# Agent attention with a squared-ReLU layer behind it: both layers, scores and transposes rewritten as pairs of 64-row matmuls

## Chip, cores and metric

The kernel runs on one core of a Trainium2 chip. The metric is device time in microseconds (us), from one launch to its end. Engines are named as in the profile: PE is TensorE's matmul stream, PEld its weight loads, DVE is VectorE, ACT is ScalarE, POOL is GpSimd, SP issues the DMAs.

## What is computed

Attention through 49 agent rows, and then a feed-forward layer on its output:

```python
a2k = sm(agents, k);  agent_v = a2k @ v          # B=4, N=12480, C=128, 49 agents
q2a = sm(q, agents);  x = q2a @ agent_v          # sm: scaled softmax along the last axis
r = np.maximum(x @ w_in, 0.0)                    # w_in 128 x 2048
out = (r * r) @ w_out                            # w_out 2048 x 128, 49920 tokens
```

All of it is float32, at float32 accuracy.

## The kernel before

**Folding.** `agent_v @ w_in` is computed once for each of the four batches (`w_make`), so that the first layer takes the 49 softmax weights of a token and not its 128 channels. Each factor is split into a high part of matmul type fp32r and the rest, low; a product is then high x high, high x low and low x high. In the program's names `hi` and `lo` are the parts of a weight, `gh` and `gl` those of the squared activation, and the columns of `pp` and `pe` hold high and low of the softmax weights side by side.

**Tiles.** Tokens come in 52 tiles of 960 (13 of each batch; `ST`), as 8 chunks of 120. The 2048 hidden columns are 16 blocks of 128 (`NF`). A step i of the main loop is one block for one tile: 832 steps, the largest part of the work.

**A step.** `mm1` forms h for two steps at once (L342-351): for each step two matmuls, one for each half of 480 tokens, over 126 rows, in which high x high, high x low and 28 of the 49 rows of low x high are stacked (L348); then, for both steps together, four matmuls over the 21 rows that are left, each in its own strip of 32 rows of the array and its own bank (L351). h of one step has two banks, 128 x 960. ACT does the ReLU (L355) and the square (L359), DVE the rounding to `gh` (L363) and the rest `gl` (L367). Four steps later (`LAG`) `mm2` adds six matmuls over 128 rows into the two banks out0 and out1, one for each half of the tokens (L378). After 16 steps `store` copies out0 on ACT (L395) and out1 on DVE (L396), and sends them out.

**Attention in between.** For a token tile: scores (L285, eight products of type float32), maximum and subtraction on DVE (L290, L294), exponential on ACT, sum and inverse on DVE (L301-305), normalisation on POOL (L308), high and low (L312, L315), eight transposes (L322), two copies on ACT (L325), and five DMAs that bring the low rows where the stacked matmuls want them (L329, L331). For the keys and values of the next batch, 13 pieces: scores (L154), copy (L158), maxima (L161), later subtraction, exponential, high, low, and the product with v (L209), which DVE adds to `acc` (L225). This work of batch b+1 lies under the main loop of batch b, so the last 208 steps have none. The work on k and v of the first batch stands ahead of the main loop, in a stage with warm-up matmuls (L495).

**Order.** Each engine runs its queue in program order. A small planner (`chain`, L418-448) gives every attention operation a step number; ties go by the written times: at step i `mm1`, then ReLU at +0.1, `mm2` of step i-4 and the store at +0.2, attention at +0.5, square +0.55, `high` +0.6, `low` +0.65, or +1.25 on even steps. The planner keeps one operation of an engine to a step, and keeps the steps in which a store falls free on ACT, DVE and PE (`taken`, L415).

**PSUM.** Eight banks: two buffers of h (two banks each), out0 and out1, and two single banks `ps_att` for attention.

Of the kernel before, what the change touches and what calls it, by code (L numbers as in the profile page):

```python
# [17 lines left out]
P = 128  # L18
# [7 lines left out]
def agent_attention_relu2_kernel(ctx: ExitStack, tc: tile.TileContext, qT, kT, v, agT, w_in, w_out, outT):  # L26
# [7 lines left out]
    C, B, NCH, _ = kT.shape  # L34
    A = agT.shape[2]
    F = w_in.shape[1]
    NF = F // P
    NS = NCH // G
    A2 = 2 * A
    scale = 1.0 / math.sqrt(C)  # L40
# [7 lines left out]
    ps_a = ctx.enter_context(tc.tile_pool(name="ps_a", bufs=2, space=bass.MemoryType.PSUM))  # L48

    ag_sb = cpool.tile([P, B, A], F32, name="ag_sb")  # L50
# [7 lines left out]
    for x in vss:  # L58
        nc.gpsimd.memset(x[:, :, C:C + 1].bitcast(F32), 1.0)
        nc.gpsimd.memset(x[:, :, C + 1:C + 2].bitcast(F32), 0.0)  # L60

# [64 lines left out]
    acc = cpool.tile([A2, VW], F32, name="acc")  # L126
    av = cpool.tile([P, 2, A], F32, name="av")
    a2 = cpool.tile([P, A2], F32, name="a2")
# [8 lines left out]
    def bank():  # L137
        turn[0] += 1
        if many[0] and turn[0] % 2:
            return ps_h.tile([P, 2, 512], F32, name="h")[:, 0]  # L140
        return ps_a.tile([P, 512], F32, name="ps_att")
# [4 lines left out]
    def k_load(b, n):  # L146
        kts[b, n] = io.tile([P, G, CH], F32, name="kt", tag="io")
        nc.sync.dma_start(out=kts[b, n], in_=kT[:, b, n * G:(n + 1) * G, :])

    def k_scores(b, n):  # L150
        kt = kts.pop((b, n))
        ps = bank()
        for c in range(G):
            nc.tensor.matmul(ps[:CH, c * A:(c + 1) * A], kt[:, c, :], ag_sb[:, b, :], start=True, stop=True)  # L154
        pss["k", n] = ps[:CH, :G * A].rearrange("p (c a) -> p c a", a=A)

    def k_copy(n):
        nc.scalar.copy(piece(n), pss["k", n])  # L158

    def k_pmax(n):  # L160
        nc.vector.tensor_reduce(out=pm[:, n, :], in_=pss.pop(("k", n)).rearrange("p c a -> p a c"), axis=AX.X, op=ALU.max)  # L161

    def k_max(step):
# [4 lines left out]
        elif step == 2:  # L168
            pss["m"] = bank()
# [3 lines left out]
        elif step == 4:  # L173
            pss["m"] = bank()
# [42 lines left out]
    def v_sum_whole(ps):  # L217
        nc.vector.tensor_copy(acc[:A, :C + 1], ps[:A, :C + 1])

    def v_sum(n):  # L220
        ps = pss.pop(("v", n))[:A2, :VW]
# [5 lines left out]
    def a_final(step):  # L227

        if step == 0:
            nc.vector.tensor_tensor(acc[:, :C], acc[:, :C], acc[:, C + 2:], op=ALU.add)  # L230
        elif step == 1:
            ps = pss["a"] = bank()
            nc.tensor.transpose(ps[:, :A2], acc[:, :C], ident[:A2, :A2])
            nc.tensor.matmul(ps[:, P:P + A2], acc[:, C:C + 1].to_broadcast([A2, P]), ident[:A2, :A2], start=True, stop=True)
# [5 lines left out]
        else:  # L240
            nc.vector.reciprocal(av[:, 1], av[:, 1])
            nc.vector.tensor_tensor(a2.rearrange("p (t a) -> p t a", a=A), av[:, 0:1].to_broadcast([P, 2, A]), av[:, 1:2].to_broadcast([P, 2, A]), op=ALU.mult)
# [5 lines left out]
    X = 28  # L248
    R = A - X
    K = A2 + X  # L250
    assert K <= P and R <= 32
    W = {}
    w_lo = cpool.tile([A, F], F32R, name="w_lo")

    def w_make(b, f, step):
        sl = slice(f * 512, (f + 1) * 512)
        if f == 0 and step == 0:
            W[b] = (wk.tile([P, F], F32R, name="w_a"), wk.tile([P, NF // 2, P], F32R, name="w_b"))
        wa, wb = W[b]
        if step == 0:  # L260
            pss["w", f] = bank()
            nc.tensor.matmul(pss["w", f][:A2, :], a2, win_sb[:, sl], start=True, stop=True)  # L262
        elif step == 1:
            nc.scalar.copy(wa[:A2, sl], pss["w", f][:A2, :])
        elif step == 2:
# [357 lines left out]
```

## Time and profile before

| | us |
|---|---|
| three runs: median (lowest to highest) | 2047.73 (2047.19 to 2049.44) |
| profiled execution: span, first to last instruction | 2044.0 |
| PE busy | 2024.0 |
| PEld busy | 1581.1 |
| DVE busy | 1823.7 |
| ACT busy | 1729.4 |
| POOL busy | 230.2 |

For the profiled execution there is its span alone; the median of the runs lies 3.7 us above it, for what is ahead of the first and behind the last instruction. A busy row is the time in which at least one instruction of the engine was under way. Matmuls overlap: a matmul of 480 columns is listed with 0.38 us, and the next may start 0.22 us after it, so that the sum of the durations is more than the time they take.

### The profile page before, as it was taken

The numbers are of one execution on the slowest core, as the hardware profiler recorded it, in microseconds if no ns is written. First come the engines' busy times: TensorE is split into PE (matmuls) and PEld (weight loads), VectorE is DVE, ScalarE is ACT, GpSimd is POOL, SyncE is SP. The second block draws the span as 40 slices with busy tenths as digits, with TensorE's granted clock in tenths as the row PEclk, the third lists the DMA queues.
The fourth block names the chain that finished last, engine by engine and source line by source line (L and its number), as shares of the span: only waits on it lengthen the run. The fifth ranks groups of instructions, "written<-read, shape, count | busy, mean of one in ns | idle before, by whom it ended". The sixth has DMA issues, their size and how long they took to land.

```text
span 2044.0 us, 30401 instructions
## 1 busy us (share of the span) xinstructions
PE 2024.0 (99%) x11011; PEld 1581.1 (77%) x11017; DVE 1823.7 (89%) x2274; ACT 1729.4 (85%) x2166; POOL 230.2 (11%) x196
## 2 busy tenths in 40 slices
PE   9899999999999999999999999999999999999999
PEld 8678777777777777777778787777777777777777
DVE  7688899999888889999998888999998988989897
ACT  2587889998887888999888888999888888888897
POOL 0100002221000001222100000122210000000000
PEclk9899999999999999999999999999999999999999
DMA  9321212211121212211112211212101111111010
GB/s 312 91 79 54 74 51 63 84 51 35 56 70 53 83 46 68 74 57 58 35 50 76 76 52 60 72 57 70 56 26 50 45 31 45 30 34 39 28 35 25
DMA packets 51446, 125.16 MB, mean 61 GB/s; under 512 B 7072, under 2 KB 16560, under 8 KB 51296
## 3 DMA queue, kind: packets, MB, share of 16 engines
q1 hardware_dynamic: 51198, 123.19, 19.5%
q8 instruction: 86, 1.41, 0.3%
q14 instruction: 64, 0.52, 0.1%
q10 hardware_dynamic: 98, 0.04, 0.0%
HBM read 81.37 MB, written 25.56 MB: 52 GB/s over the span
## 4 chain that ended last, share of the span: by engine, by line
PE 86%; DVE 8%; issue 4%; DMA 1%; ACT 1%; SPq 0%; DVEq 0%; ACTq 0%
PE out L378 51%; PE h L348 16%; PE h L351 8%; PE ps_att L154 3%; PE ps_att L285 3%; DVE gh L363 3%; DVE gl L367 2%; PE ps_att L322 1%; PE ps_att L209 1%; DVE vs L202 1%; DMA vt<-v 1%; PE ps_att L262 1%; PE h L154 0%; ACT g L359 0%; DVE ob L396 0%
## 5 line engine op out<-in xcount | busy, mean ns | idle before, releaser
L367 DVE TENSOR_TENSOR gl<-g,gh 128x960 fp32r<-128x960 f32 x832 | 1016.5, 1222 | 30.6
L355 ACT ACTIVATE r<-h 128x960 f32<-128x960 f32 x832 | 763.8, 974 | 175.9 <-PE h L351 172.2
L359 ACT ACTIVATE g<-r 128x960 f32<-128x960 f32 x832 | 825.3, 1016 | 5.2 <-DVE gl L367 5.2
L378 PE MATMUL out<-gh,wo_hi 128*128 128x480 f32 x1664 | 689.9, 415 | 5.1 <-DVE ob L396 3.6
L363 DVE CAST gh<-g 128x960 fp32r<-128x960 f32 x832 | 583.3, 701 | 97.1 <-ACT g L359 84.5
L378 PE MATMUL out<-gl,wo_hi 128*128 128x480 f32 x1664 | 633.7, 381 | 1.4 <-DVE gl L367 1.0
L378 PE MATMUL out<-gh,wo_lo 128*128 128x480 f32 x1664 | 516.1, 381 | 0.0
L348 PE MATMUL h<-p_a,w_a 126*128 126x480 f32 x1664 | 435.2, 383 | 1.8 <-ACT r L355 1.8
L378 PEld LDWEIGHTS out<-gh,wo_hi 128*128 128x128 f32 x1664 | 313.2, 188 | 141.3 <-issue 71.0
L378 PEld LDWEIGHTS out<-gh,wo_lo 128*128 128x128 f32 x1664 | 312.9, 188 | 49.3
L348 PEld LDWEIGHTS h<-p_a,w_a 126*128 126x128 f32 x1664 | 309.1, 189 | 52.8 <-ACT r L355 2.7
L378 PEld LDWEIGHTS out<-gl,wo_hi 128*128 128x128 f32 x1664 | 313.8, 189 | 41.6 <-DVE gl L367 5.7
L351 PE MATMUL h<-p_b,w_b 21*128 21x480 f32 x1664 | 204.9, 479 | 0.7 <-DMA w_b<-w_lo 0.7
L308 POOL TENSOR_TENSOR e<-e,sm 120x392 f32<-120x392 f32 x52 | 55.0, 1059 | 1322.0 <-DVE sm L305 1197.3
L351 PEld LDWEIGHTS h<-p_b,w_b 21*128 21x128 f32 x1664 | 80.1, 181 | 139.6 <-issue 137.9
L285 PEld LDWEIGHTS ps_att<-ag_sb,qt 128*120 128x120 f32 x832 | 95.2, 185 | 3.7 <-issue 0.2
L285 PE MATMUL ps_att<-ag_sb,qt 128*120 128x49 f32 x832 | 92.7, 264 | 0.0
L154 PEld LDWEIGHTS ps_att<-ag_sb,kt 128*120 128x120 f32 x704 | 80.6, 185 | 3.2 <-PE ps_att L262 0.3
L190 POOL TENSOR_TENSOR pe<-sk,pe 120x392 fp32r<-120x392 f32 x39 | 52.7, 1351 | 235.2 <-ACT pe L187 193.3
L154 PE MATMUL ps_att<-ag_sb,kt 128*120 128x49 f32 x704 | 78.4, 264 | 0.1
L158 ACT COPY sk<-ps_att 120x392 f32<-120x392 f32 x44 | 21.4, 487 | 63.7 <-PE ps_att L154 63.7
L315 POOL TENSOR_TENSOR pp<-e,pp 120x392 fp32r<-120x392 f32 x52 | 55.6, 1070 | 163.2 <-ACT pp L312 158.9
(93 smaller groups left out, 939.5 us busy)
## 6 DMA issues: line engine op xcount, KB each, us to landing
vt<-v SPq DMA_DIRECT2D x104, 243.8 KB
kt<-kT SPq DMA_DIRECT2D x52, 480.0 KB
qt<-qT SPq DMA_DIRECT2D x52, 480.0 KB
outT<-ob SPq DMA_DIRECT2D x51, 480.0 KB
p_b<-p_a SPq DMA_DIRECT2D x208, 39.4 KB
p_a<-p_a SPq DMA_DIRECT2D x52, 105.0 KB
raw<-w_in SPq DMA_DIRECT2D x4, 512.0 KB
raw<-w_out SPq DMA_DIRECT2D x4, 512.0 KB
```

Source lines behind the costliest of these rows:

```text
L154: nc.tensor.matmul(ps[:CH, c * A:(c + 1) * A], kt[:, c, :], ag_sb[:, b, :], start=True, stop=True)
L190: eng.tensor_tensor(out=pes[n][:, :, A:], in0=piece(n), in1=pes[n][:, :, :A].bitcast(F32), op=ALU.subtract)
L285: nc.tensor.matmul(ps[:CH, c * A:(c + 1) * A], qt[:, c * CH:(c + 1) * CH], ag_sb[:, s // NS, :], start=True, stop=True)
L308: eng.tensor_tensor(out=es[s], in0=es[s], in1=sms.pop(s).to_broadcast([CH, G, A]), op=ALU.mult)
L315: eng.tensor_tensor(out=pps[s][:, :, A:], in0=es.pop(s), in1=pps[s][:, :, :A].bitcast(F32), op=ALU.subtract)
L348: nc.tensor.matmul(hs[x][:, t, :TT], wa[:K, (x % NF) * P:(x % NF + 1) * P], pa[:K, t, :], start=True, stop=False)
L351: nc.tensor.matmul(hs[i + r // 2][:, r % 2, :TT], wb[rows, i % NF // 2, :], pb[rows], start=False, stop=True)
L355: nc.scalar.activation(rs_[i], hs.pop(i)[:, :, :TT], AF.Relu)
L359: nc.scalar.activation(gs[i], rs_.pop(i), AF.Square)
L363: nc.vector.tensor_copy(ghs[i], gs[i])
L367: nc.vector.tensor_tensor(out=gls[i], in0=gs.pop(i), in1=ghs[i].bitcast(F32), op=ALU.subtract)
L378: nc.tensor.matmul(o[t][:, :TT], w[:, j, :], x[:, t, :], start=st, stop=sp)
```

## The change

**First layer.** A step is now a pair of blocks for half a tile (480 tokens): `NJ` = 8 pairs, `cs` the half. The weights of the even block lie in partitions 0-48, those of the odd block in 64-112, high in `w_hi`, low in `w_lo`; the softmax weights have high in 0-48 and low in 64-112 (`p_a`), and the other way round in `p_b`. Three products, each a pair of 49-row matmuls in the two halves of the array, give the two banks of h:

```diff
-        for x in (i, i + 1):
-            hs[x] = ps_h.tile([P, 2, 512], F32, name="h")
-            for t in range(2):
-                nc.tensor.matmul(hs[x][:, t, :TT], wa[:K, (x % NF) * P:(x % NF + 1) * P], pa[:K, t, :], start=True, stop=False)
-        for r in range(4):
-            rows = slice(32 * r, 32 * r + R)
-            nc.tensor.matmul(hs[i + r // 2][:, r % 2, :TT], wb[rows, i % NF // 2, :], pb[rows], start=False, stop=True)
+        h = hs[i] = ps_h.tile([P, 2, 512], F32, name="h")
+        for x, (w, lo) in enumerate(((wh, 0), (wl, 0), (wh, 1))):
+            for u in range(2):
+                nc.tensor.matmul(h[:, u, :TT], w[ra[u], j, :], PT[s][u ^ lo][ra[u], cs, :], start=x == 0, stop=x == 2)
```

**Second layer.** Every 128-row matmul becomes two of 64 rows; the upper half of the rows is summed in out0, the lower in out1, for the same 480 tokens. A tile of the output is then 480 tokens, complete after 8 steps: 104 stores in place of 52, in which DVE adds where it copied.

```diff
+        todo = [(w, gh, e) for e in range(2) for w in (wo_hi, wo_lo)] + [(wo_hi, gl, e) for e in range(2)]
+        for x, (w, g, e) in enumerate(todo):
+            for u in range(2):
+                nc.tensor.matmul(outs[t][u][:, :TT], w[rg[u], 2 * j + e, :], g[rg[u], e, :], start=j == 0 and x == 0, stop=j == NJ - 1 and x == 5)
...
-        nc.scalar.copy(ob[:, 0, :], o[0][:, :TT])
-        nc.vector.tensor_copy(ob[:, 1, :], o[1][:, :TT])
+        nc.scalar.copy(ob, o[0][:, :TT])
+        nc.vector.tensor_tensor(ob, ob, o[1][:, :TT], op=ALU.add)
```

**Attention.** Scores (`scores`), transposes and the product with v are split by row halves in the same way; keys and queries come from DRAM laid out for it. The product with v now fills two banks, and DVE adds both to `acc`. `k_pmax` reads the copy `sk` and no longer PSUM. The low weights need no DMA, and the softmax weights two DMAs in place of five.

```diff
+    def scores(ps, x, b):
+        for c in range(H):
+            for h in range(2):
+                for u in range(2):
+                    nc.tensor.matmul(ps[:CH, u, c * A:(c + 1) * A], x[rg[u], h, c, :], ag_sb[rg[u], b, h, :], start=h == 0, stop=h == 1)
...
-            nc.tensor.matmul(pss["v", n][:A2, :VW], pe[:, c, :], vs[:, c], start=c == 0, stop=c == G - 1)
+            for u in range(2):
+                nc.tensor.matmul(pss["v", n][:A2, u, :VW], pe[rc[u], c, :], vs[rc[u], c], start=c == 0, stop=c == G - 1)
...
+        for c in range(G):
+            for u in range(2):
+                nc.tensor.matmul(pss["t", s][u][:, c, :], pp[rc[u], c, :], ident_r[rc[u], rc[u]], start=True, stop=True)
...
-        nc.sync.dma_start(out=pa[A2:K].bitcast(F32), in_=pa[:X].bitcast(F32))
-        for r in range(4):
-            nc.sync.dma_start(out=pb[32 * r:32 * r + R].bitcast(F32), in_=pa[X:A, r % 2].bitcast(F32))
+        for u in range(2):
+            nc.sync.dma_start(out=pb[ra[u]].bitcast(F32), in_=pa[ra[1 - u]].bitcast(F32))
```

**Banks and planner.** `ps_att` is one buffer of two banks in place of two of one; the planner gives it to one block of attention work at a time. Store steps stay closed to attention on ACT and DVE, and are open on PE. ReLU and `mm1` come step by step, no longer two at a time.

```diff
-    taken = {(e, s * NF + NF - 1 + LAG) for s in range(NSG) for e in ("ACT", "DVE", "PE")}
+    ends = {i for i in range(NG + LAG) if i >= LAG and (i - LAG) % NJ == NJ - 1}
+    taken = {(e, i) for i in ends for e in ("ACT", "DVE")}
...
-            at(i + (.65 if i % 2 else 1.25), low, i)
+            at(i + (1.25 if i + 1 in ends else .65), low, i)
```

Matmuls that stay over more than 64 rows: `w_make`, the steps of the key maximum and the end of a batch (`a_final`). Ahead of the main loop the warm-up matmuls take 64 rows, and nine of them go.

Below are three places in the order of instructions, with buffer numbers. First PE in the main loop before: `mm1` for two steps (h is its output; p_a, p_b and w_a, w_b its factors), and the first of the two steps of the second layer behind it.

```order
L348 MATMUL h_9214<-p_a_8760,w_a_5217 128x480 x2
L348 MATMUL h_9217<-p_a_8760,w_a_5217 128x480 x2
L351 MATMUL h_9214<-p_b_8761,w_b_5218 128x480 x2
L351 MATMUL h_9217<-p_b_8761,w_b_5218 128x480 x2
L378 MATMUL out0_9022<-gh_9133,wo_hi_92 128x480
L378 MATMUL out0_9022<-gl_9144,wo_hi_92 128x480
L378 MATMUL out1_9023<-gh_9133,wo_hi_92 128x480
L378 MATMUL out1_9023<-gl_9144,wo_hi_92 128x480
L378 MATMUL out0_9022<-gh_9133,wo_lo_93 128x480
L378 MATMUL out1_9023<-gh_9133,wo_lo_93 128x480
```

The same place of the changed kernel is PE at the start of a new output tile, behind the last of 16 transposes (L335): one step of `mm1` (L361) and the first of the twelve matmuls of `mm2` (L387).

```order
L335 MATMUL ps_att_5924<-ident_r_83,pp0_91 113x56
L361 MATMUL h_5947<-p_a_5337,w_hi_774 128x480
L361 MATMUL h_5947<-p_b_5338,w_hi_774 128x480
L361 MATMUL h_5947<-p_a_5337,w_lo_775 128x480
L361 MATMUL h_5947<-p_b_5338,w_lo_775 128x480
L361 MATMUL h_5947<-p_b_5338,w_hi_774 128x480
L361 MATMUL h_5947<-p_a_5337,w_hi_774 128x480
L387 MATMUL out0_5956<-gh_5831,wo_hi_96 128x480
L387 MATMUL out1_5957<-gh_5831,wo_hi_96 128x480
L387 MATMUL out0_5956<-gh_5831,wo_lo_97 128x480
L387 MATMUL out1_5957<-gh_5831,wo_lo_97 128x480
```

Between the last matmul on an output tile and the first on the next stood four matmuls of L348 and the four of L351; now three pairs stand there, and ahead of them in 49 of the 103 changes of tile a block of scores (L166), in 49 the 16 transposes, in 5 nothing. DVE at a store, before and then after:

```order
L363 CAST gh_8984<-g_8982 128x960
L396 COPY ob_8995<-out1_8617 128x480
L367 TENSOR_TENSOR gl_8999<-g_8982,gh_8984 128x960
L363 CAST gh_9004<-g_9002 128x960
L367 TENSOR_TENSOR gl_9006<-g_9002,gh_9004 128x960
```

```order
L373 CAST gh_12489<-g_12487 128x960
L393 TENSOR_TENSOR ob_12512<-ob_12512,out1_12267 128x480
L377 TENSOR_TENSOR gl_12516<-g_12487,gh_12489 128x960
L373 CAST gh_12539<-g_12537 128x960
L377 TENSOR_TENSOR gl_12541<-g_12537,gh_12539 128x960
```

The store's operation stays between `high` and `low` of the step ahead of it; it now needs ACT's copy besides the last matmul, and comes twice as often.

More of the change, by code (lines that the diff above doesn't have):

```diff
@@ L60, in agent_attention_relu2_kernel @@
         nc.gpsimd.memset(x[:, :, C + 1:C + 2].bitcast(F32), 0.0)
+    ppb = [cpool.tile([CH, G, AW], F32R, name=f"pp{x}") for x in range(2)]
+    for x in ppb:
+        nc.gpsimd.memset(x[:, :, A:L].bitcast(F32), 0.0)
     win_sb = cpool.tile([P, F], F32, name="win_sb")
@@ L138, in bank @@
         turn[0] += 1
-        if many[0] and turn[0] % 2:
-            return ps_h.tile([P, 2, 512], F32, name="h")[:, 0]
-        return ps_a.tile([P, 512], F32, name="ps_att")
+        if many[0] and turn[0] % 3:
+            return ps_h.tile([P, 2, 512], F32, name="h")
+        return ps_a.tile([P, 2, 512], F32, name="ps_att")
     def piece(n):
@@ L275, in agent_attention_relu2_kernel @@
     PT, qs, es, mxs, sms, pps = {}, {}, {}, {}, {}, {}
     def q_load(s):
-        qs[s] = io.tile([P, ST], F32, name="qt", tag="io")
-        nc.sync.dma_start(out=qs[s], in_=qT[:, s * ST:(s + 1) * ST])
+        qs[s] = io.tile([P, 2, H, CH], F32, name="qt", tag="io")
+        nc.sync.dma_start(out=qs[s], in_=qT[:, s])
     def q_scores(s):
-        qt = qs.pop(s)
-        ps = bank()
-        for c in range(G):
-            nc.tensor.matmul(ps[:CH, c * A:(c + 1) * A], qt[:, c * CH:(c + 1) * CH], ag_sb[:, s // NS, :], start=True, stop=True)
@@ L426, in chain @@
                 n += 1
-            need = 2 if todo[0][1] is q_transpose else 1
             t += hop[prev][todo[0][0]] if prev else 0
@@ L436, in chain @@
                     p = e
-                held = range(ts[0], ts[-1] + 2) if todo[0][0] == "PE" else ()
-                if all(banks.get(y, 0) + need <= 2 for y in held):
+                held = range(ts[0], ts[-1] + 1) if todo[0][0] == "PE" else ()
+                if not banks.intersection(held):
                     break
                 t += 1
-            for y in held:
-                banks[y] = banks.get(y, 0) + need
+            banks.update(held)
             for (e, f, *args), g in zip(todo, ts):
@@ L448, in chain @@
         return first, t
-    reads_bank = (k_copy, k_pmax, k_max, v_sum, a_final, w_make, q_max, q_sub, q_copy)
+    reads_bank = (k_copy, k_max, v_sum, a_final, w_make, q_shift, q_copy)
     def plan_tokens(s, base, loaded=False):
-        first, end = chain(base, [("PE", q_scores, s), ("DVE", q_max, s), ("DVE", q_sub, s), ("ACT", q_exp, s), ("DVE", q_sum, s), ("DVE", q_inverse, s),
+        first, end = chain(base, [("PE", q_scores, s), ("DVE", q_shift, s), ("ACT", q_exp, s), ("DVE", q_inverse, s),
                                 ("POOL", q_norm, s), ("ACT", q_hi, s), ("POOL", q_lo, s),
-                                ("PE", q_transpose, s), ("ACT", q_copy, s, 0), ("ACT", q_copy, s, 1)])
+                                ("PE", q_transpose, s), ("ACT", q_copy, s)])
         if not loaded:
@@ L494, in warm_up @@
         for _ in range(n):
-            nc.tensor.matmul(wps, warm[:, :P], warm, start=True, stop=True)
+            nc.tensor.matmul(wps, warm[:L, :P], warm[:L], start=True, stop=True)
     def begin():
@@ L571, in agent_attention_relu2_kernel @@
     at(t + 9, begin)
[L572 to L574 removed]
     for f in range(2, F // 512):
[L576 to L577 removed]
+        banks.clear()
+        chain(f - 2, [("PE", w_make, 0, f, 0), ("ACT", w_make, 0, f, 1), ("DVE", w_make, 0, f, 2)])
+    banks.clear()
+    plan_tokens(1, 2, True)
     for s in range(2, NSG):
[L579 removed]
+        plan_tokens(s, (s - 2) * NF + LAG + NJ - 1)
     for b in range(1, B):
```

209 lines of the change are left out of this document (91 added, 118 removed).

## The prediction

> **What bounds the kernel now.** I read the busy times and the chain of waits on the page first.
>
> ```profile
> PE 2024.0 (99%) x11011; PEld 1581.1 (77%) x11017; DVE 1823.7 (89%) x2274; ACT 1729.4 (85%) x2166; POOL 230.2 (11%) x196
> ...
> PE 86%; DVE 8%; issue 4%; DMA 1%; ACT 1%; SPq 0%; DVEq 0%; ACTq 0%
> ```
>
> PE is busy for 2024.0 of 2044.0 us and carries 86% of the chain; DVE and ACT follow at 89% and 85%. So the end is set by how fast PE goes through its own stream, and two engines are not far behind it. Whether PE really streams in its 99% is seen from one turn of the main loop (two steps), in the timeline of PE and PEld; columns are start, length, engine, line and count.
>
> ```profile
> 2028.08 0.48 PE L378 MATMUL out<-gh,wo_hi 128*128 128x480 f32 x1
> 2028.40 0.38 PE L378 MATMUL out<-gl,wo_hi 128*128 128x480 f32 x1
> 2028.40 0.19 PEld L378 LDWEIGHTS out<-gh,wo_hi 128*128 128x128 f32 x1
> 2028.62 0.38 PE L378 MATMUL out<-gh,wo_hi 128*128 128x480 f32 x1
> ...
> 2030.81 1.02 PE L348 MATMUL h<-p_a,w_a 126*128 126x480 f32 x4
> ...
> 2031.77 0.19 PEld L351 LDWEIGHTS h<-p_b,w_b 21*128 21x128 f32 x4 [0.33 <-issue]
> 2031.77 0.49 PE L351 MATMUL h<-p_b,w_b 21*128 21x480 f32 x4
> ...
> 2032.18 0.19 PEld L378 LDWEIGHTS out<-gh,wo_hi 128*128 128x128 f32 x1 [0.23 <-issue]
> 2032.18 0.48 PE L378 MATMUL out<-gh,wo_hi 128*128 128x480 f32 x1
> ...
> 2032.50 0.38 PE L378 MATMUL out<-gl,wo_hi 128*128 128x480 f32 x1
> ```
>
> A turn takes 2032.18 - 2028.08 = 4.10 us. From the second matmul of L378 (2028.40) to the first of L348 (2030.81) lie 11 matmuls of 480 columns in 2.41 us: 0.219 us each, which I call a slot. The load for the next matmul starts with the one that runs and is done in 0.19, so it is hidden. Sixteen full matmuls would take 3.50 us; the four of L351 thus cost 0.60, though they start together and load together. Before them no load runs for 0.33 us, behind them for 0.23. The list of waits shows the same gaps over the whole run:
>
> ```profile
> PEld h L351 <- issue: 137.9, 415, 0.6
> ...
> PEld out L378 <- issue: 71.8, 314, 0.3
> ```
>
> It is 415 times 0.33 and 314 times 0.23 us: PE empties itself each time it goes from matmuls of many rows to matmuls of strips, and back.
>
> **The main loop on PE.** A turn after the change has the same work as 18 pairs: two steps of three pairs in `mm1` and six in `mm2`. If a pair takes one slot, that is 18 x 0.219 = 3.94 us in place of 4.10, or 0.16 less; 416 turns give -66 us. One slot is the value I take, since the four of L351 show it: the four of L348 start within 1.02 - 0.38 = 0.64 us, 0.21 apart, the last at 2031.45; from there to the load of L351 go 0.32 us, 0.21 of stream and 0.11 to drain; from their load to the next load 0.41, which leaves, less 0.10 of load (below) and the same 0.11, some 0.20 for four streams at once. What the trace does not show is such strips in a row, with the next weights loaded under them. Bounds: a stream with no gap at all is 0.200 us, as the matmuls while the clock stood at half speed were 0.400 apart;
>
> ```profile
> 88.31 0.60 PE L378 MATMUL out<-gh,wo_hi 128*128 128x480 f32 x1
> 88.71 0.60 PE L378 MATMUL out<-gl,wo_hi 128*128 128x480 f32 x1
> ```
>
> and if the 0.019 between 0.200 and 0.219 had to be paid by each half of a pair, it is 0.238. On 7488 pairs (9 x 832) each nanosecond is 7.5 us, so these ends lie 142 us to either side.
>
> Here a rule speaks against the change. The Trainium skill, page "TensorE: Matmul & The Clock Gate", section "Part 3: Packing small matmuls — row/col tiling", says that a weight load runs beside a matmul only if the two use different row groups. In the rows above it doesn't hold: the load at 2028.40 has all 128 rows, starts with the matmul of 128 rows and costs the stream nothing. By the rule a pair would pay its load, some 0.10 us, behind each stream, and the sum would be +749 us; by the rows it pays nothing, and I go by the rows.
>
> **Attention on PE.**
>
> ```profile
> 1006.05 1.78 PE L285 MATMUL ps_att<-ag_sb,qt 128*120 128x49 f32 x16
> 1007.65 0.46 PE L378 MATMUL out<-gh,wo_hi 128*128 128x480 f32 x1
> ...
> L322 PE MATMUL ps_att<-ident_r,pp 120*98 120x120 f32 x412 | 42.7, 246 | 0.0
> ...
> 336.03 0.82 PE L322 MATMUL ps_att<-ident_r,pp 120*98 120x120 f32 x8
> ...
> 0.00:40.00 40.00, 36.49 (x292) 31.86 (x297) 24.92 (x53) 9.65 (x18) 0.86 (x10) 1.00 0.97 326
> ```
>
> A block of scores is 16 passes (two for each of the eight float32 products) in 1.60 us: 0.10 each, for a moving side of 49 columns only, so it is the load of 120 columns that is paid. After the change there are 32 passes, in 16 pairs. The four loads of L351 within 0.19 us say that different row groups load side by side, so I take 1.60 again, or nothing. One after the other it would be 3.2, +1.6 for each of the 52 + 39 blocks in the main loop: +146 (the 13 of the first batch lie where the DMA share is 0.97). The transposes stand 0.082 apart, (0.82 - 0.25)/7, for 98 columns of weights; with 113 it is an estimated 0.095 and eight pairs cost 0.1 us more: 52 x 0.1 = +5. The product with v stays at eight streams of 258 columns: nothing. In `w_make`, `k_max` and `a_final` some 7 places a batch still use more than 64 rows, which cost no switch before and now cost one there and back, at most the 0.38 that L351 cost beyond a slot (0.60 - 0.22): 3 x 7 x 0.38 = +8.
>
> **Stores.** A tile of the output now ends 104 times, with DVE behind ACT, and its banks must be empty before `mm2` goes on.
>
> ```profile
> L396 DVE COPY ob<-out 128x480 f32<-128x480 f32 x13 | 8.5, 652 | 0.6 <-PE out L378 0.6
> L395 ACT COPY ob<-out 128x480 f32<-128x480 f32 x13 | 7.2, 554 | 0.7 <-PE out L378 0.7
> ```
>
> (These are of the window 500-1000 us.) The last result lands 0.38 - 0.22 = 0.16 us behind its slot, then 0.55 and 0.65: out1 is free 1.36 us after PE left it. Three pairs of `mm1` cover 0.66. In 49 changes scores add 1.60 and cover it; in 49 the transposes add 0.76, together 1.42, just enough if ACT takes the copy at once; it does not always, so I put 0.1 us on each of these: +5. If ACT came 1 us late every time, it would be +49.
>
> **DVE and ACT.** The window 500-1000 holds just one batch: 208 steps.
>
> ```profile
> 500.00:1000.00 500.00, 497.83 (x2712) 389.76 (x2710) 453.32 (x559) 434.76 (x550) 66.14 (x52) 1.00 0.20 60
> ...
> L367 DVE TENSOR_TENSOR gl<-g,gh 128x960 fp32r<-128x960 f32 x208 | 256.7, 1234 | 7.6
> L359 ACT ACTIVATE g<-r 128x960 f32<-128x960 f32 x208 | 207.8, 1018 | 1.8 <-DVE gl L367 1.8
> L355 ACT ACTIVATE r<-h 128x960 f32<-128x960 f32 x208 | 191.0, 975 | 39.6 <-PE h L351 38.7
> ...
> L363 DVE CAST gh<-g 128x960 fp32r<-128x960 f32 x208 | 146.0, 702 | 23.8 <-ACT g L359 21.1 <-PE out L378 2.6
> ...
> L225 DVE TENSOR_TENSOR acc<-ps_att,acc 98x258 f32<-98x258 f32 x11 | 4.6, 418 | 0.0
> ...
> L266 DVE TENSOR_TENSOR w_lo<-ps_att,w_a 49x512 fp32r<-49x512 f32 x4 | 2.7, 677 | 0.9 <-ACT w_a L264 0.9
> ```
>
> DVE is busy for 453.3 us of it. The change adds 13 store operations at 0.65 (8.5) and doubles the width of 13 sums into `acc`: between nothing and 0.42 each; I take 0.26 (3.4), the difference of 0.68 for 512 columns (L266) and 0.42 for 258. The halves of `w_make` give under 1. That is 466. ACT gets 13 x 0.55 more: 442. PE goes from 500 to 500 - 104 x 0.16 = 483.4, with transposes and switches near 487. So DVE would be busy in 96%, where it has 91% now, and its 46.7 idle us must shrink to about 21. Most of that is waiting for work that PE paces (21.1 for ACT's square, and ACT in turn 38.7 for h), and goes when PE is faster. But a store now makes DVE wait for the last matmul and for ACT, ahead of a `low` that could have run: that is forced idling, twice a tile. With all 46.7 kept a batch would take 512.7; with what PE's pace explains gone, 487. Between 0 and 25 us a batch I take 4, since the product waits four steps for its operand and a delay of a microsecond or two is absorbed: +16.
>
> The small DMAs for the low weights and three of five for each tile go from SP's queue; the DMA share in the window is 0.20, so nothing is gained or lost there. Fewer warm-up matmuls and other order at the start: at most a few us to either side, taken as nothing.
>
> The sum: -66 + 5 + 8 + 5 + 16 = -32, from a span of 2044.0 to 2012. The median of the runs is 3.7 above the span, so I forecast 2016 us.
>
> **Rivals.**
> - DVE becomes the bound (slower). The mechanism is the one above: forced idling at 26 stores a batch. It decides from 34 us of idle time a batch on (500 - 466), where all of PE's gain is gone; the four batches at 512.7 give +51 us, 2099, and half way, at 500, it is no change. For it: 96% leaves little play, and the store order. Against: ReLU and square now come one step at a time, and DVE can lag a few us before PE misses an operand. Chance of slower this way 0.14, of no change 0.08. The Trainium skill, page "TensorEngine Tiling (Array Packing)", section "PSUM Bottleneck", warns of this: tiling speeds up the matmuls and not the emptying of PSUM. The rows agree as far as DVE's 453.3 of 500 shows.
> - A pair costs more than a slot (slower). From 4.3 ns a pair (32/7.5) the forecast gain is gone. At 0.238 it is +142, 2158. Against it stands the 0.20 us left for four streams. Chance 0.08.
> - Loads of the two halves follow each other in blocks of scores: +146, 2162. Against it: the four loads of L351 started together. Chance 0.07.
> - A pair costs less than a slot (faster): the gaps of one half filled by the other. At 0.200 PE would need 142 less, but DVE then holds the batch between its 466 and my 487 + 4 + 1 = 492: at 478, 22 less than now, it is -88 in four batches, 1960. Against it: 0.219 has the load hidden already, so that it isn't plain what would fill. Chance 0.08.
> - No load is hidden under a pair: +749, 2765. Chance 0.02; it is the rule of the page named above.
> - My forecast, with 1985 to 2040 as its own range (store and stall terms from nothing to twice, a pair 2 ns to either side): 0.53.
>
> **The numbers.** Forecast 2016. The range leaves out the pair at 0.238, serial loads and no hidden load (0.17) and little at the low end: 1965 to 2100, with the DVE-bound case inside. The three runs before spread over 0.1%, so about 0.2% (4 us) is what can be told from no change. Faster 0.53 + 0.08 = 0.61; same 0.08; slower 0.14 + 0.08 + 0.07 + 0.02 = 0.31.
>
> **What would show it.** In the profile after: the gaps "issue" ahead of loads of the first layer gone; L387's pairs starting 0.219 apart, both halves at about the same time (0.238 or staggered at 0.3: the sum is wrong); a turn of two steps at 3.94 us with no attention; blocks of scores at 1.6 us (3.2: serial); PE idle ahead of the first matmul of an output tile, on DVE L393 or ACT L392, of the order of 5 us; DVE busy at 95% or more of a batch, and PE idle on `gl` of the order of 16 us in all. I am wrong if PE's idle time passes 50 us, with DVE's `gl` or the store named for it, or if turns are longer than 4.0.

## The result and the profile after

The changed kernel takes 2121.14 us, the median of 4 runs (2115.72 to 2126.22), beside 2048.59 us (2047.19 to 2050.60, 4 runs) for the kernel before: a ratio of 1.035, 95% interval 1.033 to 1.037. It is slower by 73 us where 32 less were forecast, and lies outside the range. The profiled execution has a span of 2113.9 us. Busy times and chain of the page after:

```profile
PE 2038.3 (96%) x20056; PEld 1872.4 (89%) x20056; DVE 1884.9 (89%) x2345; ACT 1801.0 (85%) x2234; POOL 248.4 (12%) x199
...
PE 79%; DVE 10%; ACT 6%; issue 5%; DMA 0%; DVEq 0%; SPq 0%; ACTq 0%
```

PE was the bound at 99%; now it has 3% more idle time, and DVE and ACT have a larger part of the chain. First, what the change was made of: PE in the timeline, near the end of the main loop and at a block of scores.

```profile
2003.25 0.38 PE L387 MATMUL out<-gh,wo_hi 64*128 64x480 f32 x1
2003.25 0.38 PE L361 MATMUL h<-p_a,w_hi 49*128 49x480 f32 x1
2003.47 0.38 PE L387 MATMUL out<-gh,wo_lo 64*128 64x480 f32 x1
...
2005.19 0.38 PE L387 MATMUL out<-gh,wo_hi 64*128 64x480 f32 x1
...
614.96 0.20 PE L166 MATMUL ps_att<-ag_sb,qt 64*120 64x49 f32 x1
...
616.56 0.46 PE L361 MATMUL h<-p_a,w_hi 49*128 49x480 f32 x1
```

A step of nine pairs takes 1.94 us here, 0.216 a pair, so a pair holds its slot and two steps take some 3.9 in place of 4.10. A block of 32 score passes takes 616.56 - 614.96 = 1.60. At these places the pairs do what the sum put in for them; the 73 us are elsewhere, and the first part of them is the start. Rows of PE, after and then before:

```profile
40.97 3.66 PE L166 MATMUL h<-ag_sb,kt 64*120 64x49 f32 x31
...
98.55 0.46 PE L361 MATMUL h<-p_a,w_hi 49*128 49x480 f32 x1
...
108.76 2.02 PE L275 MATMUL ps_att<-win_sb,a 128*113 128x512 f32 x2 [7.44 <-DVE w_lo L282]
...
120.70 0.63 PE L387 MATMUL out<-gh,wo_hi 64*128 64x480 f32 x2
```

```profile
74.53 1.26 PE L348 MATMUL h<-p_a,w_a 126*128 126x480 f32 x4
...
85.75 0.77 PE L378 MATMUL out<-gh,wo_hi 128*128 128x480 f32 x1
```

The second layer starts at 120.70 instead of 85.75: 35 us later. Twenty-four of them stand already at the first layer, and the block of scores at 40.97 takes twice the time of the one above: PE runs at half speed there. The other part is in the main loop: from its first matmul of L387 to the end of the span it is 1993.2 us, from L378 before 1958.3, again 35 more, though the turns give 66 back. So some 101 us are lost there. Its windows, with the sums (before's in a fence of its own):

```profile
120.00:500.00 380.00, 366.83 (x3716) 335.22 (x3714) 347.08 (x420) 333.95 (x423) 58.90 (x43) 0.97 0.23 64
500.00:1000.00 500.00, 483.75 (x4864) 449.70 (x4864) 457.01 (x562) 435.62 (x548) 66.86 (x50) 0.98 0.22 61
1000.00:1500.00 500.00, 483.98 (x4867) 449.05 (x4865) 456.58 (x562) 436.87 (x549) 65.69 (x49) 0.98 0.21 61
1500.00:2000.00 500.00, 490.09 (x4750) 450.48 (x4748) 460.10 (x567) 464.05 (x551) 43.56 (x34) 0.99 0.14 41
sum 1880.00, PE 1824.65 PEld 1684.45 DVE 1720.76 ACT 1670.49 POOL 235.01; mean PE 456.16 PEld 421.11 DVE 430.19 ACT 417.62 POOL 58.75
...
L377 DVE TENSOR_TENSOR gl<-g,gh 128x960 fp32r<-128x960 f32 x202 | 249.3, 1234 | 16.6
```

```profile
sum 1880.00, PE 1873.46 PEld 1461.46 DVE 1704.13 ACT 1640.09 POOL 220.42; mean PE 468.36 PEld 365.36 DVE 426.03 ACT 410.02 POOL 55.11
```

PE stands idle for 1880 - 1824.65 = 55 us instead of 7, so 49 more. The column behind POOL is the granted clock, 0.97, 0.98, 0.98 and 0.99, where the window of before in the prediction has 1.00. The trace's record of the clock gives it more exactly: 67 us at half speed lie in these windows, so 34 us are lost. With the 13 that the forecast gave to transposes and switches, that is 49 + 34 + 13 = 96 of the 101. The row of `gl` (window 500-1000) counts 202 steps in 500 us, so a batch of 208 takes 515 us.

The waits of PEld, PE and ACT name the place:

```profile
PEld out L387 <- DVE ob L393: 67.1, 52, 3.2
...
PE out L387 <- DVE ob L393: 48.4, 44, 2.9
...
ACT r L365 <- PE h L361: 192.1, 184, 4.8
```

One such wait, in the timeline of all engines:

```profile
432.71 0.58 ACT L392 COPY ob<-out 128x480 f32<-128x480 f32 x1
...
433.06 0.65 DVE L373 CAST gh<-g 128x960 fp32r<-128x960 f32 x1
...
433.81 1.16 DVE L377 TENSOR_TENSOR gl<-g,gh 128x960 fp32r<-128x960 f32 x1
...
434.89 0.69 DVE L217 TENSOR_TENSOR vs<-vt,vs 120x512 fp32r<-120x512 f32 x1
...
435.49 0.65 DVE L373 CAST gh<-g 128x960 fp32r<-128x960 f32 x1
...
436.06 0.65 DVE L393 TENSOR_TENSOR ob<-ob,out 128x480 f32<-128x480 f32 x1
...
436.76 0.77 PE L387 MATMUL out<-gh,wo_hi 64*128 64x480 f32 x1 [2.94 <-DVE ob L393]
...
438.93 0.60 PE L361 MATMUL h<-p_a,w_hi 49*128 49x480 f32 x1
...
439.33 0.57 PE L361 MATMUL h<-p_b,w_hi 49*128 49x480 f32 x1
...
439.73 0.40 PE L361 MATMUL h<-p_b,w_lo 49*128 49x480 f32 x1
...
440.38 0.98 ACT L365 ACTIVATE r<-h 128x960 f32<-128x960 f32 x1 [3.48 <-PE h L361]
```

ACT has emptied its bank at 433.29, but DVE first works off the rest of a rounding, its low part, a piece of the values and the next rounding before it comes to the store, and PE stands for 2.9 us. Then its pairs are 0.40 apart until 439.73, half speed for some 3 us, and ACT, which lives on PE's h, is idle for 3.5. By the Trainium skill, page "TensorE: Matmul & The Clock Gate", section "Part 1: The HAM clock gate (the "warmup" mystery)", the clock is halved after an idle window of about 3.4 us and comes back after a busy one. The trace agrees with the length: between 123 and 2000 us its record of the clock has 15 stretches at half speed, eleven of 3.4 us and four of 6.8. It does not show that PE must be idle so long: each stretch begins in, or up to 1.6 us behind, such a wait for DVE's `ob`, and these waits are 0.8 to 2.9 us long. Not every wait brings one; behind that of 2.26 us that ends at 1035.18 there is none.

Why DVE is late there: windows of 50 us, before (the first in the key phase, the others where the values are summed) and after (values).

```profile
150.00:200.00 50.00, 50.00 (x291) 40.10 (x289) 41.48 (x52) 39.35 (x48) 2.11 (x2) 1.00 0.20 66
...
350.00:400.00 50.00, 48.88 (x265) 37.80 (x265) 49.24 (x60) 44.53 (x60) 11.43 (x9) 1.00 0.19 56
400.00:450.00 50.00, 49.82 (x264) 38.40 (x262) 49.14 (x59) 45.97 (x62) 14.92 (x11) 1.00 0.25 75
```

```profile
350.00:400.00 50.00, 45.01 (x413) 41.07 (x414) 45.15 (x56) 41.25 (x55) 8.22 (x6) 0.90 0.26 68
```

A batch isn't one stage. In its value phase DVE was busy for 49.2 of 50 us before the change, in its key phase for 41.5, and the 91% of the batch that the prediction used is a mean of both. In the value phase it had no room for a faster PE, nor for the change's own additions.

A full DVE is not the whole of it. In the last 208 steps, which have no work on keys and values, most of the pairs' gain is gone as well: the row of `gl` for the window 1670-2030 counts 166 steps before and 167 after. PE is listed as busy for 356.6 of these 360 us, at a clock of 1.00. Most of this loss does not show as idle time, because a matmul is listed with 0.38 us and the next may start 0.22 us after it: the first 0.16 us of a wait count as busy.

### The profile page after: what moved, and what is told of

Its sections match the earlier page's. It is cut to its first block, busy times and chain, and to the rows that moved or that the text cites. A ratio compares the mean times of both kernels' runs of the same rounds, so it can differ in the third digit from the quotient of the medians.

```text
span 2113.9 us, 48363 instructions
## 1 busy us (share of the span) xinstructions
PE 2038.3 (96%) x20056; PEld 1872.4 (89%) x20056; DVE 1884.9 (89%) x2345; ACT 1801.0 (85%) x2234; POOL 248.4 (12%) x199
## 4 chain that ended last, share of the span: by engine, by line
PE 79%; DVE 10%; ACT 6%; issue 5%; DMA 0%; DVEq 0%; SPq 0%; ACTq 0%
PE out L387 45%; PE h L361 22%; PE ps_att L166 6%; DVE gh L373 3%; ACT r L365 2%; DVE gl L377 2%; PE ps_att L225 2%; PE h L166 2%; ACT g L369 2%; DVE ob L393 1%; PE ps_att L335 1%; DVE vs L217 1%; PE ps_att L275 1%; ACT ob L392 0%; PE out L486 0%
## 5 line engine op out<-in xcount | busy, mean ns | idle before, releaser
L387 PE MATMUL out<-gh,wo_hi 64*128 64x480 f32 x3328 | 852.2, 385 | 48.4 <-DVE ob L393 48.4
L387 PE MATMUL out<-gh,wo_lo 64*128 64x480 f32 x3328 | 841.8, 383 | 0.0
L387 PE MATMUL out<-gl,wo_hi 64*128 64x480 f32 x3328 | 656.7, 383 | 0.0
L387 PEld LDWEIGHTS out<-gh,wo_hi 64*128 64x128 f32 x3328 | 566.0, 187 | 95.4 <-DVE ob L393 67.1
L361 PE MATMUL h<-p_a,w_hi 49*128 49x480 f32 x1664 | 648.2, 391 | 0.0
L387 PEld LDWEIGHTS out<-gh,wo_lo 64*128 64x128 f32 x3328 | 568.7, 189 | 21.1
L361 PE MATMUL h<-p_b,w_hi 49*128 49x480 f32 x1664 | 548.7, 391 | 0.0
L387 PEld LDWEIGHTS out<-gl,wo_hi 64*128 64x128 f32 x3328 | 457.5, 187 | 26.1
L361 PEld LDWEIGHTS h<-p_a,w_hi 49*128 49x128 f32 x1664 | 312.7, 188 | 21.4 <-ACT r L365 4.6
L361 PE MATMUL h<-p_a,w_lo 49*128 49x480 f32 x832 | 316.8, 381 | 0.0
L361 PE MATMUL h<-p_b,w_lo 49*128 49x480 f32 x832 | 316.7, 381 | 0.0
L361 PEld LDWEIGHTS h<-p_b,w_hi 49*128 49x128 f32 x1664 | 303.4, 188 | 11.4 <-DMA p_b<-p_a 0.2
L361 PEld LDWEIGHTS h<-p_b,w_lo 49*128 49x128 f32 x832 | 158.4, 190 | 4.9
L361 PEld LDWEIGHTS h<-p_a,w_lo 49*128 49x128 f32 x832 | 158.4, 190 | 4.5
L166 PEld LDWEIGHTS ps_att<-ag_sb,qt 64*120 64x120 f32 x1632 | 104.5, 184 | 5.9 <-issue 3.3
L166 PE MATMUL ps_att<-ag_sb,qt 64*120 64x49 f32 x1632 | 102.1, 264 | 2.9 <-DVE w_lo L282 2.7
```

Of the source, the lines that this page charges most:

```text
L166: nc.tensor.matmul(ps[:CH, u, c * A:(c + 1) * A], x[rg[u], h, c, :], ag_sb[rg[u], b, h, :], start=h == 0, stop=h == 1)
L361: nc.tensor.matmul(h[:, u, :TT], w[ra[u], j, :], PT[s][u ^ lo][ra[u], cs, :], start=x == 0, stop=x == 2)
L387: nc.tensor.matmul(outs[t][u][:, :TT], w[rg[u], 2 * j + e, :], g[rg[u], e, :], start=j == 0 and x == 0, stop=j == NJ - 1 and x == 5)
```

## Experiments

Times are medians; each run has its own runs of the kernel before beside it, 2048 to 2049 us, and ratios are against these. Three names stand in the expectations: A says that matmuls of half height don't raise the clock, F that VectorE has no room in the value phases and is late wherever PE meets it, G that two such meetings, store and attention bank, make up the loss.

**The start.** Full-height warm-ups in the changed kernel, and half-height ones in the kernel before:

```diff
-            nc.tensor.matmul(wps, warm[:L, :P], warm[:L], start=True, stop=True)
+            nc.tensor.matmul(wps, warm[:, :P], warm, start=True, stop=True)
```

> The changed kernel with the warm-up matmuls over 128 rows again, nothing else. Theory A (matmuls that fill half of the array do not bring the clock up, so the start runs at half speed): the matmuls ahead of the main loop stand 0.22 us apart soon after the start, a block of scores there takes 1.6 us in place of 3.5, the first matmul of the second layer starts near 86-95 us in place of 120.7, and the time is about 25 to 35 us lower, 2085 to 2095 us. Rival B (the pairs themselves, their memory layout or the DMAs make the start longer): the start stays near 120 us and the time near 2120.

> The kernel before with its warm-up matmuls over 64 rows, nothing else. Theory A (half of the array does not bring the clock up): here the scores of the start still use 128 rows with 49 moving columns, so the clock stays down for part of the start only or for all of it; the main loop starts 10 to 35 us later than at 85.8 us and the time is 2058 to 2083 us. Rival B (the pairs or the layout of the changed kernel): no change, 2048 within 4 us.

2102.73 (1.0265, 1.025 to 1.028), 18 less than the changed kernel; and 2077.61 (1.0148, 1.012 to 1.017), 29 more than before. The first rows of the first layer:

```profile
78.92 0.46 PE L361 MATMUL h<-p_a,w_hi 49*128 49x480 f32 x1
```

```profile
101.02 1.25 PE L348 MATMUL h<-p_a,w_a 126*128 126x480 f32 x4
```

Against 98.55 and 74.53 the lines of the same name move by -20 and +26. So warm-up matmuls over 64 rows, which use one half of the array, do not bring the clock up, whichever kernel they stand in. The trace's record of the clock agrees: its first full speed stands at 64 us in the changed kernel and at 69 in the kernel before with half-height warm-ups, at 5 us in the other two. (Ahead of its first record a window reads 1.00.) The wait of 7.4 us for `w_lo` at the start stays, and with it the way from the first layer to the second: 22.15 us in the changed kernel, the same with full warm-ups, 11.2 before.

**The store's banks.** First, ACT empties both banks and DVE adds in SBUF. Second, DVE does its addition without reading a bank (the upper half of the rows is left out of the result). Third, the first layer of the next step goes ahead of the first second-layer matmul of a tile.

```diff
         nc.scalar.copy(ob, o[0][:, :TT])
-        nc.vector.tensor_tensor(ob, ob, o[1][:, :TT], op=ALU.add)
+        nc.scalar.copy(oc, o[1][:, :TT])
+        nc.vector.tensor_tensor(out=ob, in0=ob, in1=oc, op=ALU.add)
```

```diff
+        nc.vector.tensor_tensor(ob, ob, ob, op=ALU.add)
```

```diff
-            at(i, mm1, i)
+            at(i - .85 if i - 2 in ends else i, mm1, i)
```

> The changed kernel with a store in which ACT copies both banks to SBUF and DVE adds there: the banks no longer wait for DVE's queue; DVE does as many additions as before, ACT gets 104 more copies of 0.56 us (+58 us of work, in 1801 of 2114). Theory C (PE waits at a new output tile for the addition, which stands behind late work in DVE's queue, and runs at half clock after the longest of these waits): PE's idle time for the store falls from about 115 us (PE and PEld together) to under 30, the clock stays at 0.99 or above, and the time falls by 40 to 90 us, to 2030 to 2080. Rival D (DVE's throughput is the bound, the store only the place where it shows): the wait turns up ahead of the second layer on gl, the time stays at 2100 to 2125. Rival E: ACT becomes the late one; PE waits for ACT's copies, 2100 or more.

> The changed kernel with DVE adding ACT's copy to itself in place of out1: the upper half of the second layer's rows is left out of the result. DVE's work and its wait for ACT stay as they are; only PE's wait for DVE at a new output tile is gone. Theory C (that wait and the half clock behind it): -70 to -110 us, 2010 to 2050, with the start as long as before. Rival D (DVE's throughput): PE waits on gl, above 2100.

> The changed kernel with the first layer of one more step issued ahead of the first second-layer matmul of a new output tile: 0.66 us more of cover for each of the 103 changes of tile, no other change. Rival C (a wait of 0.5 to 3 us at each store): 0.5 to 0.66 us less at most changes of tile, 40 to 60 us in all, 2060 to 2080. Theory F (DVE full in the value phase, about half of the steps): the cover helps outside of it, where the waits are about 0.5 us each, and inside it the wait returns elsewhere: 15 to 30 us, 2090 to 2105.

2098.26, 2083.18 and 2090.56 (1.0251, 1.0171 and 1.0203, each within 0.002): 23, 38 and 31 less than the changed kernel. In the second the window 1670-2030 holds 171 steps where the changed kernel has 167, so the store's wait is what takes the gain of the last 208 steps. In the first two PE waits no more for DVE's part of the store, but at the next place, the single attention buffer, which DVE empties (the list of waits of the second):

```profile
PE ps_att L225 <- DVE e L301: 37.1, 12, 4.4
```

**DVE's load.** Keys in 36% and values in 64% of a batch's steps instead of half and half; the values' low parts left out (their share of the result is missing), 78 operations and 57 us of DVE; and a combination: uneven, full warm-ups, both banks emptied by ACT, the addition on POOL.

```diff
+        dk, dv = 0.36 * (span - 46) / NS, 0.64 * (span - 46) / NS
```

```diff
-        eng.tensor_tensor(out=vs[:, :, C + 2:], in0=vts[n][:, halves[h], :C], in1=vs[:, :, :C].bitcast(F32), op=ALU.subtract)
```

```diff
+        nc.gpsimd.tensor_tensor(out=ob, in0=ob, in1=oc, op=ALU.add)
```

> The changed kernel with the planner giving the keys 36% and the values 64% of a batch's steps, in place of half and half: the same work, spread so that a value piece (about 2.2 us of DVE) gets more room than a key piece (about 0.85). Theory F (DVE is full in the value phase, which it was at 98% before the change; there every us of its lateness reaches PE through the output and attention banks): PE's waits on DVE's store addition fall from 115 us (PE and PEld) to about half, the clock drops in that phase become rare, and the time falls by 30 to 60 us, to 2060 to 2090. Rival C (each store has a wait of its own, whatever DVE's load): waits and time stay, 2115 to 2125.

> The changed kernel without the low part of the values (DVE's 78 subtractions of 0.73 us, 57 us in all, 52 of them under the main loop by way of three batches; the low columns hold zeros, so that part of the product is left out). Nothing else moves. Theory F (DVE full in the value phase): 57 us less of DVE work there gives back as much or more in time, since waits and half clock go with it: 2045 to 2075. Rival C (waits of the store by themselves): at most 20 us less, 2100 or more.

> All that the theories name, mended together: warm-up matmuls over 128 rows (about -18 by its own run), ACT copies both output banks and POOL adds them in SBUF (DVE loses 68 us of work, ACT gains 58), keys and values at 36% and 64%. Theory F: PE waits little on DVE; start 19 us shorter, main loop near PE's own 1.97 us a step: 2121 - 18 - 90 = about 2010, 2000 to 2040, faster than the kernel before. If POOL's additions slow DVE, or ACT becomes late (1801 + 58 us): 2050 to 2090.

2132.61 (1.041), 2071.83 (1.0103) and 2102.17 (1.0258). Less work gives 49 us back, and the store's waits shrink with it (from 48.4), though nothing was done to the store:

```profile
PE out L387 <- DVE ob L393: 24.2, 35, 1.5
```

Spreading missed: the store's wait of PE grew to 69.3 us. Why isn't known: PE was busy for 231.7 of the 250 us from 250 to 500, where the changed kernel has 237.2, so the loss lies in the very phase that got more room. The combination missed as well, with 51 us of L225's waits and POOL busy for 417 us.

**The attention bank.** Bank and store were taken for two meetings that must go together (theory G): a bank is held one step longer by the planner behind `q_shift`. This is tried with the addition that reads no bank; alone; with both banks emptied by ACT and full warm-ups; and with these, the first layer ahead and the last of the output weights made some steps later.

```diff
-                held = range(ts[0], ts[-1] + 1) if todo[0][0] == "PE" else ()
+                held = range(ts[0], ts[-1] + 1 + any(x[1] is q_shift for x in todo[:n])) if todo[0][0] == "PE" else ()
```

> As the run in which DVE does not read the output bank (the upper half of the second layer's rows is left out), and the planner keeps the attention banks one step longer behind token scores, before it gives them to the product with v. Theory G (PE meets DVE at two places with hardly any room, the output banks and the attention banks; DVE is late by a few us whenever attention work bunches, and each meeting turns that into idle PE): the 37 us that PE waited there for DVE's subtraction go, too: 2083 - 30 to 45 = 2038 to 2053. Rival F (DVE's throughput is the bound in the value phase): a third place appears, PE waits on gl: 2075 to 2085.

> The changed kernel with the attention banks kept one step longer behind token scores, nothing else. Theory G: the store's meeting comes first and hides this one (7 us of PE's waits are for it now): 2105 to 2121. If the single pair of attention banks were the root, 2080 to 2095.

> ACT copies both output banks and DVE adds in SBUF, attention banks one step longer, warm-up over 128 rows; the full result. Theory G: 2098 - 18 - 25 to 40 = 2040 to 2055. Rival F: 2075 to 2085.

> As the kernel before this one in the list, and the first layer one step ahead at a new output tile, and the last quarter of the output weights made some steps later, out of the way of the folded weights at the start. Theory G: 10 to 15 us less at the start (PE waits 7.4 + 2.7 us there for DVE's w_lo, at half clock), a few us at the changes of tile: 2020 to 2040, faster than the kernel before by up to 1%. Rival F: 2055 to 2075.

2097.04, 2116.16, 2092.98 and 2087.38 (1.0237, 1.0326, 1.0232, 1.0194). Holding the bank only moves the wait again, to the scores behind a value sum: the first of the four is 14 us slower than the same without the held bank. The first of the four, waits and a window of 10 us behind one:

```profile
PE ps_att L166 <- DVE acc L241: 29.3, 6, 5.1
```

```profile
370.00:380.00 10.00, 9.65 (x70) 8.67 (x72) 7.09 (x10) 3.64 (x5) 0.00 (x0) 0.57 0.45 124
```

DVE is left idle only behind such a stop of PE (7.1 of 10, clock 0.57). Theory G fell: mended meetings do not add up.

**The ledger.** The low parts issued behind the next high part, which takes away DVE's gap of 0.08 us ahead of each; then the three single costs taken away at once (full warm-ups, no bank read by DVE, no low values; the result lacks the same parts as there); the best full version with the low parts moved; and that with the key maximum read from the bank.

```diff
-            at(i + (1.25 if i + 1 in ends else .65), low, i)
+            at(i + 1.62, low, i)
```

```diff
-        nc.vector.tensor_reduce(out=pm[:, n, :], in_=piece(n).rearrange("p c a -> p a c"), axis=AX.X, op=ALU.max)
+        nc.vector.tensor_reduce(out=pm[:, n, :], in_=pss.pop(("k", n)).rearrange("p u c a -> p a u c"), axis=AX.XY, op=ALU.max)
```

> The changed kernel with the low part of every step's result issued one step later on VectorE, behind the next step's high part, so that it never follows directly on the high part that it reads. Theory F (VectorE has no room in the value phases: 0.08 us stands idle before each of 832 low parts, 69.6 us in all, and this is capacity that VectorE lacks): the idle time before the low parts falls from 69.6 to under 40 us, the time falls by 20 to 50, to 2070 to 2100. Rival H (the gaps are only VectorE running level with ScalarE and lie where there is slack; the time is set by the store's meeting of the three engines): 2110 to 2125 and the waits on the store's addition stay near 115 us.

> The changed kernel with full-height warm-ups, the store's second bank unread (the upper half of the rows is left out of the result) and the values' low parts left out: half-height warm-ups, a bank that waits for VectorE's queue, and VectorE's load are taken away together. Theory F (these three are where the forecast gain of 66 went): single savings were 18, 38 and 49; if they add up, 2016 and, as each takes part of the same idle time, 2005 to 2035, with the clock granted over 0.99. Rival J (there is a further cost in the row-half pairs that the load of VectorE has nothing to do with): 2050 or more.

> The version of the changed kernel with ScalarE emptying both output banks, attention banks held, full-height warm-ups and the first layer ahead (2087), and the low parts behind the next high parts. Theory F: 2045 to 2070. Rival H: 2080 to 2090.

> The same and the maximum over the keys read from the attention bank again instead of from SBUF (0.56 instead of 0.85 us, 48 times, and it no longer waits for ScalarE's copy to be readable). Theory F: 5 to 15 under the version without it. Rival H: no difference.

The first: 2112.24 (1.031), as the rival expected. DVE got its gaps back and used them to wait for ACT:

```profile
L377 DVE TENSOR_TENSOR gl<-g,gh 128x960 fp32r<-128x960 f32 x832 | 1014.8, 1220 | 0.0
L373 DVE CAST gh<-g 128x960 fp32r<-128x960 f32 x832 | 580.9, 698 | 159.7 <-ACT g L369 149.1 <-PE out L387 6.1
```

So DVE's raw capacity isn't the whole; what is left as the reason is that it is late at a place where PE has no slack. The second: 2020.89 (0.9856, 0.983 to 0.988), under the kernel before. The three savings were 18, 38 and 49, 105 together; at once they give 100. Its window and count of steps:

```profile
500.00:1000.00 500.00, 493.38 (x5087) 464.52 (x5086) 462.66 (x562) 457.32 (x579) 69.16 (x52) 1.00 0.23 64
...
L377 DVE TENSOR_TENSOR gl<-g,gh 128x960 fp32r<-128x960 f32 x212 | 260.9, 1231 | 19.6 <-PE out L387 0.5
```

212 steps in 500 us are 491 us a batch at a clock of 1.00, where the prediction worked out 492. No large further cost lies in the pairs. Two things limit what it shows. It leaves out work that the kernel before does, and the kernel before without that work was not run, so being under it is no gain of the pairs alone. And its five runs lie from 2014.49 to 2039.15; the profile is of the longest, in which PE fell to half speed at 11 us, in spite of the full warm-ups, and stayed there for 51 us, in scores and single warm-ups.

The last two are 2089.60 and 2096.45 (1.0198 and 1.0247). The third came out as its rival expected, the fourth above both, and the list of waits of the third names one place for it:

```profile
PE ps_att L335 <- POOL pp L327: 51.2, 9, 5.9
```

**GpSimd.** These nine waits are for an instruction that takes 1.5 us in the median and 11.2 at these places. The same version, timeline:

```profile
359.70 11.20 POOL L327 TENSOR_TENSOR pp<-e,pp 120x392 fp32r<-120x392 f32 x1 [3.51 <-ACT pp L324]
...
367.72 0.65 DVE L395 TENSOR_TENSOR ob<-ob,oc 128x480 f32<-128x480 f32 x1
368.29 0.65 DVE L373 CAST gh<-g 128x960 fp32r<-128x960 f32 x1
368.86 1.15 DVE L377 TENSOR_TENSOR gl<-g,gh 128x960 fp32r<-128x960 f32 x1
...
370.95 1.72 PE L335 MATMUL ps_att<-ident_r,pp 64*113 64x64 f32 x16 [5.77 <-POOL pp L327]
```

DVE runs without a gap until 370.0, and POOL is done 0.9 us later; so it is at all nine. By the Trainium skill, page "SBUF — State Buffer", section "SBUF: two separate sides", the two share a pair of ports: a GpSimd instruction, or a VectorE one with two inputs in SBUF when the GpSimd one reads SBUF, locks it for its whole length, and the other is blocked. The rows agree, and add that a DVE without gaps can keep POOL out over many instructions; no run tests the ports by themselves. In the run with the low parts moved alone the longest is 6.3 us, in the changed kernel 2.1. So closing DVE's gaps had bought a new wait. Two runs plan PE's transposes, then also its value sums (with a third buffer for the values), further behind POOL:

```diff
+        hop["POOL"]["PE"] = 9 if s > 1 else 3
```

```diff
-            _, end = chain(max(t1 + 3, t2 + 2), [("PE", v_acc, n), ("DVE", v_sum, n)])
+            _, end = chain(max(t1 + 6, t2 + 2), [("PE", v_acc, n), ("DVE", v_sum, n)])
```

> The version with both output banks emptied by ScalarE, attention banks held, full-height warm-ups, the first layer ahead and the low parts behind the next high parts (2090), whose TensorE waits 9 times, 51 us in all, in the transposes for GpSimd's low part of the probabilities, an instruction that mostly takes 1.5 us and nine times about 11 us while VectorE works without a gap; here the plan puts the transposes 9 steps instead of 3 behind that instruction (from the second tile on), so that TensorE no longer meets it. Theory K (a VectorE without gaps keeps GpSimd out, which is why mending VectorE's gaps gained nothing): the 51 us and the half clock behind them go, 2020 to 2045, under the kernel before. Rival L (as with each mend so far, another engine is late next): 2070 or more with a new wait in the transposes' place.

> The version with the transposes later (2060) with the value sums, too, planned 6 instead of 3 steps behind GpSimd's low part of the exponentials, and three instead of two buffers for the values so that the next pieces may be written meanwhile. Its largest wait, of TensorE's value sums for GpSimd (21 us, 6 times, up to 4.6), should go. Theory K: 2025 to 2045, under the kernel before (2049). Rival L: 2055 or more, with a new wait.

2059.77 (1.0047, 1.003 to 1.006) and 2052.06 (1.0018, 1.0006 to 1.0029, 12 runs beside 17 of before at 2049.04). Theory K had the direction, and both came out 7 us or more above its numbers; no large wait stands in the second (the largest of PE's in the main loop follow below). It is the best version with the full result: level with the kernel before to about 0.2%, not faster.

```profile
PE h L361 <- DMA p_b<-p_a: 12.2, 17, 1.1
PE h L361 <- ACT r L365: 11.0, 8, 2.4
...
L377 DVE TENSOR_TENSOR gl<-g,gh 128x960 fp32r<-128x960 f32 x208 | 253.8, 1220 | 0.0
```

208 steps in the window 500-1000: the batch of the kernel before. This version has all of DVE's work still, so much of its lateness can be covered by planning further ahead, together with the other changes that this version has. What parts it from the ledger run's 491 us a batch (DVE's 57 us for the values, ACT's second copy, small waits like these) was not separated.

## Why the prediction failed, point by point

- **The turn**, -66: right. Pairs hold the slot, and a stretch of the ledger run gives the batch that was worked out, 491 against 492 us. The rivals on the pair's price and on loads that aren't hidden are out.
- **Scores**, nothing: right, 1.60 us a block. **Transposes and switches**, +13: not measured singly; the ledger leaves no room for much more.
- **The start**, "at most a few us to either side, taken as nothing": failed, +35. About 20 are half-height warm-ups that leave the clock low (shown in both kernels); 7.4 and 2.7 are PE's waits for the one attention buffer behind `w_lo`; the last 5 were not taken apart.
- **Stores**, "0.1 us on each of these: +5": failed. Its working let ACT be late, but assumed DVE at hand. DVE came up to 3 us late, behind a step and a half of its own queue: PE stood 48 us there. The bound of +49 matches that by luck, since it was for a late ACT at each of 49 places, and it lacked the sequel: behind 15 of the stops PE runs at half speed for 3.4 or 6.8 us, and ACT and DVE run dry behind it. That is the 34 us of clock.
- **DVE and ACT**, "between 0 and 25 us a batch I take 4": failed, and here lies the wrong reading. The window of 500 us was taken as one stage of 91%; it is a value phase at 98% and a key phase with room. The rival "DVE becomes the bound" comes nearest: it gave 512.7 us a batch, measured were 515. Its price of +51 counted four such batches. Only three have work on keys and values; the loop got 35 us longer, and the start's 35 make up the rest. Its mechanism is half right: DVE waited 41 us for ACT's copy at stores, but the loss lies in PE, which waits there for DVE. Of the two names, load and lateness, the runs speak for lateness at meetings without slack: the last 208 steps lose the gain without the load, and planning further ahead, on top of the other mends, makes good most of it with the load still there, while closing DVE's gaps alone doesn't. Load is what makes the waits long (-49 without the values' low parts).
- Together: -66 + 13 for the work, 35 for the start, 48 for PE's waits at stores and 34 of clock are +64 of the 73 measured.
- The sign that the prediction named for being wrong, more than 50 us of idle PE with the store named for it, is what the profile showed: 55 us, with 48 for the store.

Open: the last 9 us of that sum, why the uneven split made it worse, and what holds the best full version 31 us above the ledger run.

## What to carry to other kernels

Before you count on a faster engine, cut the window into the stages of the work and look at the next engine's share in each: 91% over a batch was 98% in its value phase. Where a change adds a place at which the fast engine needs a nearly full engine's queue, price its lateness by what stands in that queue ahead, and add the half-speed stretch that can follow a stop. Compare steps per window and not only busy time, which hides short waits of PE. Mending one such meeting shows the next; a run that takes all suspected costs away at once tells whether the list is near complete.

## What the runs showed of the hardware

- Warm-up matmuls over 64 of 128 rows do not raise PE's speed: they cost the kernel before 29 us, and full ones gave the changed kernel 18. The block of scores at 40.97 took 3.66 us; with full warm-ups such a block takes 1.88. The granted clock of the window 40 to 60 us reads 1.00 all the same, as its record begins only at 64 us. Pairs of 480 columns that fill both halves do bring the speed back: the 15 stretches at half speed in the main loop last 3.4 or 6.8 us.
- Pairs of 64-row and 49-row matmuls kept up one slot of 0.216 us for 480 columns (nine in 1.94), with all weight loads hidden.
- The maximum over a strided piece took 0.85 us from SBUF (x52), where it took 0.56 from a bank before; the version that reads the bank again was no faster.
- A POOL instruction of 1.5 us took 11.2 beside a DVE without gaps, nine times in one run.
